# Four staging tiles instead of two for the first eight quarters of V, two of them on the still unused bytes of C

## The chip, the cores and the metric

The kernel runs on one core of one Trainium2 chip. The metric is device time in microseconds (us) of one execution, lower is better. "Faster" or "slower" needs 2%. Where a smaller difference is called one, the 95% interval of its ratio leaves out 1.

The profile names the engines so: PE is TensorE (PEld its weight loads), DVE is VectorE, ACT is ScalarE, POOL is GpSimd, SP is SyncE, which only issues transfers. "ACTq" and "SPq" are transfers being issued by the sequencers of ACT and SP. The "granted clock" is the share of TensorE's full clock that the profile says it was given.

## The reference, cut to what matters

Two independent blocks, each on a sequence of 2048 x 1024, are computed and put side by side: a state-space recurrence (A), and attention over segments with a memory (B). Only one product matters here, V of block B:

```python
def _B_ref(x, mem0, Wq, Wk, Wv, Wo, seg_len):      # x: 1 x 2048 x 1024, 32 heads of 128
    ...
        v = jnp.einsum('btd,dhe->bhte', h, Wv)      # V: 1024 x 4096 weights
    ...
```

and of block A, that its output needs the matrix C, a second 1024 x 1024 complex product, only after the whole recurrence input has been computed:

```python
    Bu = jnp.einsum('bld,pd->blp', x + 0j, B_bar)
    ...                                             # the recurrence over 2048 steps
    y = 2.0 * jnp.einsum('blp,dp->bld', hseq, Cmat).real + x * Dskip[None, None, :]
```

## The kernel before

V is computed first, in 8 blocks of four heads (`hb`), each in four quarters (`q`) of 512 rows. A quarter is four tiles of 128 rows; a tile is eight accumulating matmuls of 128x512 into one PSUM buffer (where TensorE leaves its results). ScalarE copies ("evicts") the four tiles into a staging tile in SBUF (the memory on the core), and one DMA then writes the staging tile to DRAM (`b_vx`), from where attention reads it much later.

```python
    def ps(self, tag, shape=(128, 512), dt=FP32):
        ...  bufs={"P": 3, "S": 2, "R": 1, "O": 2, "U": 2}[tag]     # three PSUM buffers "P"

    def stage_init(self):
        self.vst = []
        for i in range(2):
            self.vst.append(self.wl.tile([128, 4, 4, EW], BF16, name=f"b_vst{i}", bufs=1))
            self.k.G.memset(self.vst[i][:, :, :, E:EW], 1.0)
        self.nst = 0

    def next_st(self):
        self.nst += 1
        return self.vst[self.nst % 2]

    def v_x(self, hb, q, w):
        ...
        st = self.next_st()
        ...
        for i in range(4):
            ...
                p = k.ps("P")[:]
                self.v_mm(p, w, 4 * q + i)                          # 8 matmuls
            k.copy("v" if first and i % 2 else "s", st[:, i, :, 0:E], p.rearrange(...))   # "s": ScalarE
        ...
        Q.dma_start(vx[s0:s0 + n * 128, :].rearrange(...), st[:, 0:n, :, :].rearrange(...))
        ...
```

The order of the first work items is V quarters (0,0), (1,0), (0,1), (1,1), with nothing between them; from then on one step of the state-space block (16 matmuls into a "U" buffer, 3.45 us of TensorE) stands between two quarters in most places. While the first V quarters run, ScalarE also builds sine and cosine tables for the state-space block, and SP loads `x` of both blocks by transposing DMAs.

The staging tile of quarter n is that of quarter n-2. So the first eviction of a quarter has two conditions: TensorE must have finished the tile, and the DMA that wrote quarter n-2 to DRAM must have landed.

The space for C is a tile of its own, `a.CT` (named `t32`, in the profile `t`), 32 KB per partition. It is allocated at the start and written from 208 us on.

## Time and profile before

| | before |
|---|---|
| time, median of 3 | 1247.49 us (1247.30 to 1248.05) |
| span of the profiled execution | 1245.6 us |
| TensorE busy | 1234.4 us, 99% |
| ScalarE busy | 263.5 us, 21% |
| DMA share, 20 to 40 us | 1.17 to 1.24 |
| granted TensorE clock | 1.000 |

The DMA share is the mean busy share of the 16 DMA engines. The times of all packets are added up, so a share above 1, as here, means that packets overlapped on an engine.

From the page of the kernel before: the span, the busy line, and the chain of work that ended last by engine.

```profile
span 1245.6 us, 20120 instructions
...
PE 1234.4 (99%) x8270; PEld 662.3 (53%) x8342; DVE 668.0 (54%) x1250; ACT 263.5 (21%) x631; POOL 275.8 (22%) x407
...
PE 98%; DMA 1%; issue 0%; ACT 0%; POOL 0%; DVE 0%; SPq 0%; ACTq 0%
```

The timeline of TensorE in the stretch of the change (start, length, engine, line, operation, output<-inputs, sizes, number of instructions; idle time before a group would stand at the end in brackets):

```profile
15.20 20.92 PE L64 MATMUL psP<-b_wv,b_xe 128*128 128x512 bf16 x94
35.96 3.62 PE L64 MATMUL psU<-a_xT,a_bt 128*128 128x512 bf16 x16
39.41 7.07 PE L64 MATMUL psP<-b_wv,b_xe 128*128 128x512 bf16 x31
```

Twelve V tiles, 96 matmuls (two records are missing), start at 15.20 us, and the next group starts at 35.96: 20.76 us, 216 ns per matmul, 1.73 us per tile, no bracket anywhere. A group's printed length (20.92) reaches past the start of the next group because matmuls are pipelined and their ends are modelled; the starts are what to subtract.

The timeline of ScalarE around the fourth quarter (L89 is the copy helper, L494 the issue of the write):

```profile
24.96 0.57 ACT L89 ACTIVATE b_vst<-psP 128x512 bf16<-128x512 f32 x1
25.43 0.62 ACT L238 ACTIVATE a_tabh<-a_tabh 128x512 bf16<-128x512 bf16 x1
25.56 0.37 ACTq L494 DMA_DIRECT2D b_vx<-b_vst  x1
...
30.20 0.37 ACTq L494 DMA_DIRECT2D b_vx<-b_vst  x1
32.75 1.08 ACT L89 ACTIVATE b_vst<-psP 128x512 bf16<-128x512 f32 x2 [1.97 <-PE psP L64]
...
39.43 0.37 ACTq L494 DMA_DIRECT2D b_vx<-b_vst  x1
```

At 25.56 us the write of the second quarter is issued. The first eviction of the fourth quarter, which goes into the same staging tile, starts at 32.75 us after 1.97 us of idle ScalarE. The bracket blames TensorE, but TensorE had finished that tile at about 15.20 + 9 x 1.73 = 30.8 us, and an eviction that waits only for TensorE starts within about 0.2 us of the end of its tile. So the other condition, the landing of the write, must have been the late one. That is a reading.

TensorE's own waits up to 200 us (waiter, what it waited for, us in total, times, longest):

```profile
PE psR L64 <- DVE hpb L105: 1.3, 1, 1.3
PE psP L64 <- ACT b_xe L89: 0.2, 1, 0.2
```

Neither is an eviction of V.

### The profile page before, as it was taken

How to read it: one execution, taken by the hardware profiler on the slowest of the kernel's cores; microseconds unless marked ns; L12 is line 12 of the kernel's file. 1: busy time of each engine (PE TensorE's matmuls, PEld its weight loads, DVE VectorE, ACT ScalarE, POOL GpSimd, SP SyncE). 2: the span in 40 equal slices, each digit the busy share in tenths (PEclk: the TensorE clock that was granted, in tenths of full speed). 3: DMA queues.
4: the chain of work that ended last, by engine and by line, in shares of the span. 5: the costliest groups of instructions: out<-in, count | busy, mean ns of one | idle time of the engine just before them, and what ended most of it. 6: DMA issues, size and time to landing. Idle time of an engine off the chain costs nothing.

```text
span 1245.6 us, 20120 instructions
## 1 busy us (share of the span) xinstructions
PE 1234.4 (99%) x8270; PEld 662.3 (53%) x8342; DVE 668.0 (54%) x1250; ACT 263.5 (21%) x631; POOL 275.8 (22%) x407
## 2 busy tenths in 40 slices
PE   9999999999999999999999999999999999999998
PEld 5444444444455555556666656555665554446444
DVE  4688899998711124666666666666666641001000
ACT  5344444443310000211112111111211110000000
POOL 4111331212332321322222222222222220000000
PEclk9999999999999999999999999999999999999999
DMA  9965444554898834664454544545473289407000
GB/s 245 272 192 148 131 132 128 144 156 107 241 323 247 251 116 95 192 167 123 95 144 108 144 108 114 138 92 133 96 155 95 61 223 220 110 18 153 17 17 27
DMA packets 316022, 176.83 MB, mean 142 GB/s; under 512 B 138650, under 2 KB 301326, under 8 KB 315926
## 3 DMA queue, kind: packets, MB, share of 16 engines
q1 hardware_dynamic: 293830, 147.95, 48.1%
q10 hardware_dynamic: 21072, 24.38, 5.9%
q0 software_dynamic: 1024, 3.17, 0.7%
q8 instruction: 66, 1.08, 0.4%
q14 instruction: 30, 0.25, 0.1%
HBM read 89.14 MB, written 53.17 MB: 114 GB/s over the span
## 4 chain that ended last, share of the span: by engine, by line
PE 98%; DMA 1%; issue 0%; ACT 0%; POOL 0%; DVE 0%; SPq 0%; ACTq 0%
PE psP L64 82%; PE psU L64 9%; PE psS L64 3%; PE psO L64 2%; PE psR L64 2%; DMA wo<-in_B_Wo_dram 1%; DMA b_xr<-in_B_x_dram 0%; ACT b_xe L89 0%; POOL b_m L644 0%; DVE b_ost L91 0%; SPq L64 0%; ACT b_e L641 0%; ACTq L89 0%
## 5 line engine op out<-in xcount | busy, mean ns | idle before, releaser
L64 PE MATMUL psP<-b_xe,b_wq 128*128 128x480 bf16 (+1 forms) x1280 | 247.7, 343 | 0.1
L64 PE MATMUL psP<-b_xe,b_wk 128*128 128x480 bf16 (+1 forms) x1280 | 247.7, 343 | 0.0
L64 PE MATMUL psP<-b_wv,b_xe 128*128 128x512 bf16 (+2 forms) x1033 | 223.4, 372 | 1.0 <-ACT b_xe L89 0.2
L644 POOL TENSOR_TENSOR b_m<-b_e,maskB 99x396 bf16<-99x396 bf16 x160 | 139.8, 874 | 334.0 <-ACT b_e L641 334.0
L641 ACT ACTIVATE b_e<-psS 99x396 bf16<-99x396 f32 x176 | 88.2, 501 | 532.2 <-PE psS L64 527.9
L64 PEld LDWEIGHTS <-b_wk 128*128 128x128 bf16 x1280 | 119.4, 98 | 94.2
L64 PEld LDWEIGHTS <-b_wq 128*128 128x128 bf16 x1280 | 118.7, 98 | 87.7
L64 PEld LDWEIGHTS <-b_xe 128*128 128x128 bf16 x1056 | 101.8, 98 | 119.1 <-ACT b_xe L89 0.4
L91 DVE CAST b_k<-psP 128x480 bf16<-128x480 f32 (+1 forms) x192 | 97.5, 529 | 101.1 <-PE psP L64 101.1
L91 DVE CAST b_q<-psP 128x480 bf16<-128x480 f32 (+1 forms) x192 | 97.5, 529 | 93.0 <-PE psP L64 91.4
L64 PEld LDWEIGHTS <-b_ol 128*128 128x128 bf16 x864 | 84.3, 98 | 94.4
L64 PE MATMUL psU<-a_xT,a_bt 128*128 128x512 bf16 x493 | 113.9, 379 | 1.1
L64 PE MATMUL psP<-t,a_hl 128*128 128x512 bf16 x496 | 112.1, 379 | 0.8
L91 DVE CAST b_ost<-psP 128x512 bf16<-128x512 f32 (+1 forms) x17 | 11.5, 676 | 183.4 <-PE psP L64 182.4
L64 PE MATMUL psP<-wo,b_ol 128*128 128x512 bf16 (+1 forms) x440 | 91.9, 364 | 0.4
L64 PE MATMUL psP<-t,b_ol 128*128 128x512 bf16 x408 | 91.7, 379 | 0.4
L280 POOL TENSOR_SCALAR a_tt<-a_pr,a_tabf 128x1 f32<-128x1 f32 x48 | 34.1, 709 | 243.5 <-DVE a_pr L275 243.5
L89 ACT ACTIVATE b_vst<-psP 128x512 bf16<-128x512 f32 x126 | 72.0, 589 | 71.0 <-PE psP L64 65.0
L661 DVE TENSOR_TENSOR b_ob<-psO,b_accR 99x384 bf16<-99x384 f32 x160 | 85.9, 553 | 2.0
L267 DVE TENSOR_TENSOR a_pr<-psU,a_tabf 128x2048 f32<-128x2048 f32 x32 | 73.0, 2282 | 15.7 <-PE psU L64 14.0
L64 PEld LDWEIGHTS <-a_bt 128*128 128x128 bf16 x512 | 49.2, 98 | 57.6
L64 PEld LDWEIGHTS <-a_hl 128*128 128x128 bf16 x512 | 49.1, 98 | 56.7
(200 smaller groups left out, 963.8 us busy)
## 6 DMA issues: line engine op xcount, KB each, us to landing
b_v<-b_vx SPq DMA_DIRECT2D x16, 1122.0 KB
b_wv<-in_B_Wv_dram SPq DMA_DIRECT2D x16, 1024.0 KB
b_on<-b_ob SPq DMA_DIRECT2D x15, 960.0 KB
b_vx<-b_vst ACTq DMA_DIRECT2D x24, 544.0 KB
a_hs<-a_h SPq DMA_DIRECT2D x32, 256.0 KB
b_wog<-in_B_Wo_dram SPq DMA_DIRECT2D x4, 2048.0 KB
b_wq<-in_B_Wq_dram SPq DMA_DIRECT2D x16, 512.0 KB
b_wk<-in_B_Wk_dram SPq DMA_DIRECT2D x16, 512.0 KB
```

The costliest lines, as they stand in the source:

```text
L64: r = f(*a, **kw)
L89: self.S.activation(out, in_, ACT.Copy)
L91: self.V.tensor_copy(out, in_)
L267: V.tensor_tensor(pr[:], u[:].unsqueeze(1).to_broadcast([128, 2, 2, TB]), view(t3, [[TB + 1, 2], [TB + 1, 2], [1, TB]]), ALU.mult)
L280: G.tensor_scalar(tt[:, j:j + 1], w[:, j, TB - 1:TB], t3[:, 1, TB:TB + 1], None, ALU.mult)
L641: k.S.activation(e[:], s[0:GW, :, :, 0:GW], ACT.Exp, scale=float(E) ** -0.5, accum_out=self.accE[0:GW, i:i + 1])
L644: k.G.tensor_tensor(m[0:GW, 0:4 * GP].rearrange("p (a b q) -> p a b q", a=2, b=2)[:, :, :, 0:GW], e[:], mask[0:GW, :, :].unsqueeze(2).to_b ...
L661: V.tensor_tensor(self.ob[:, b0:b0 + n, :], o[0:GW, 0:n, 0:E], r.unsqueeze(2).to_broadcast([GW, n, E]), ALU.mult)
```

## The change

Its intent: the early evictions of V shall not wait for the writes of earlier quarters. Two more staging tiles would not need new space: the bytes of C lie idle until long after the first eight quarters. So the first quarters rotate over four tiles, two of them views of C, and from the eighth on over the old two.

```diff
-    def stage_init(self):
-        self.vst = []
-        for i in range(2):
-            self.vst.append(self.wl.tile([128, 4, 4, EW], BF16, name=f"b_vst{i}", bufs=1))
-            self.k.G.memset(self.vst[i][:, :, :, E:EW], 1.0)
+    def stage_init(self, ct):
+        self.vst = [self.wl.tile([128, 4, 4, EW], BF16, name=f"b_vst{i}", bufs=1)[:] for i in range(2)]
+        spare = [ct[:, 1, 4 * i:4 * i + 3, :].rearrange("p c d -> p (c d)")[:, 0:16 * EW].rearrange("p (i h e) -> p i h e", i=4, h=4)
+                 for i in range(2)]
+        self.sts = self.vst + spare
+        for st in self.sts:
+            self.k.G.memset(st[:, :, :, E:EW], 1.0)
         self.nst = 0
     def next_st(self):
         self.nst += 1
-        return self.vst[self.nst % 2]
+        return self.sts[self.nst % (4 if self.nst < 8 else 2)]
...
-            b.stage_init()
+            b.stage_init(a.CT)
```

(One more line, cut here, drops a `[:]` where the two old tiles are used again later.) The instructions of TensorE, VectorE, ScalarE and SP keep their order, apart from those that only wait; GpSimd gets two more memsets.

More of the change, by code (lines that the diff above doesn't have):

```diff
@@ L728, in load_o_early @@
         elif q == 2:
-            t = [v[:].rearrange("p i h e -> p (i h e)")[:, 0:2048].rearrange("p (h n) -> p h n", h=4) for v in self.vst]
+            t = [v.rearrange("p i h e -> p (i h e)")[:, 0:2048].rearrange("p (h n) -> p h n", h=4) for v in self.vst]
         else:
```

## The prediction

> **What bounds the kernel now.** TensorE. The busy table gives PE 1234.4 us of a 1245.6 us span (99%), granted clock 1.00; the chain that ended last is 98% PE. Where the change acts, the PE timeline is one unbroken stream: from 15.20 to 35.96 us twelve V tiles of eight 128x512 matmuls, 20.76 us for 96 matmuls, 216 ns each, and the same pace on to 100 us. The Trainium skill ("TensorE: Matmul & The Clock Gate", "Back-to-back issue gap") states this pace for back-to-back 128x512 matmuls, so no stall hides inside the modelled "busy". PE's waits up to 200 us are 1.3 us at the warm-up and 0.2 us for ScalarE's copy of x; none names a staging tile.
>
> **What the change removes.** An eviction of V into a staging tile waits until the DMA that last read it has landed: with two tiles that of the quarter before last, with four (first eight quarters) four back. By the instruction orders, PE, DVE, ScalarE and SP keep theirs; only waits differ. ScalarE's timeline shows where the wait bites: the fourth quarter's first eviction starts at 32.75 us after 1.97 us idle. Its PSUM was complete at about 30.8 us, and evictions elsewhere start 0.2 us after the last matmul, so about 1.75 us is the write issued at 25.56 us, which took about 7.1 us to land. The page charges the idle to PE. The third quarter starts right behind its predecessor on ScalarE (26.03), the fifth to eighth 0.2 us after PE. So one wait of 1.75 us goes, off PE.
>
> **Is it on the critical path?** No. There are three "P" PSUM buffers. The late eviction frees its buffer at 33.3 us; PE needs it for that quarter's fourth tile at 29.08 + 3 x 1.73 = 34.3 us. 1 us of slack is left, and PE shows no gap. The gain is 0, or a few tenths in an execution where that write lands over 1 us later.
>
> **What it adds.** Two GpSimd memsets (0.21 us each) before the iota, which then ends near 5.8 instead of 5.43 us; its reader on DVE starts at 6.37 us behind a copy, with 2.5 us idle after it. Cost 0. The transposed load of C into those bytes gets waits on ScalarE and GpSimd work of the first 70 us, but is issued after 200 us. Cost 0. Bytes moved: unchanged.
>
> The Trainium skill ("DMA: Bandwidth & Descriptors", "Anatomy of one DMA") puts most of a DMA's fixed cost of about 2 us into completion. Here a staging write took about 7 us while the DMA share is over 1.0 (20 to 40 us): the reuse wait is real, but not binding.
>
> **Predicted.** 1247.4 us, within 1246.5 to 1248.5; chances: faster by over 2% 0.01, within 2% 0.98, slower 0.01.
>
> **What would show each step.** Right: the fourth quarter's first eviction starts near 31.0 us, ScalarE's idle before it near 0.2 us; the PE timeline from 15 to 100 us is the same to 0.1 us; the span is within 0.5 us of 1245.6. Wrong: a new PE wait on a "psP" buffer, or twelve tiles taking other than 20.76 us.
>
> **What would make it wrong.** The profiled execution hiding a stall that timed ones have (their spread is only 0.75 us), or a shifted DMA colliding with the loads of x at 30 to 50 us.

## The result, and the profile after

| | before | after |
|---|---|---|
| time, median of 4 | 1247.47 us (1247.30 to 1248.05) | 1247.18 us (1246.98 to 1247.52) |
| span of the profiled execution | 1245.6 us | 1245.5 us |
| TensorE busy | 1234.4 us | 1234.3 us |
| ratio after / before | | 0.9997 (95%: 0.9980 to 1.0014) |

A ratio here is the mean time of one kernel's runs over that of the other's runs of the same rounds, so it is not quite the ratio of the medians.

From the page of the kernel after, the lines shown of before:

```profile
span 1245.5 us, 20119 instructions
...
PE 1234.3 (99%) x8270; PEld 662.2 (53%) x8342; DVE 667.7 (54%) x1250; ACT 263.6 (21%) x631; POOL 276.2 (22%) x409
```

TensorE's timeline after:

```profile
14.99 20.92 PE L64 MATMUL psP<-b_wv,b_xe 128*128 128x512 bf16 x94
35.75 3.62 PE L64 MATMUL psU<-a_xT,a_bt 128*128 128x512 bf16 x16
39.20 7.07 PE L64 MATMUL psP<-b_wv,b_xe 128*128 128x512 bf16 x31
```

ScalarE's timeline after (the write's line is L496 now; `t` is a staging tile on the bytes of C):

```profile
24.75 0.58 ACT L89 ACTIVATE t<-psP 128x512 bf16<-128x512 f32 x1
...
25.35 0.37 ACTq L496 DMA_DIRECT2D b_vx<-t  x1
...
29.99 0.37 ACTq L496 DMA_DIRECT2D b_vx<-t  x1
30.77 0.60 ACT L89 ACTIVATE b_vst<-psP 128x512 bf16<-128x512 f32 x1 [0.20 <-PE psP L64]
32.50 0.60 ACT L89 ACTIVATE b_vst<-psP 128x512 bf16<-128x512 f32 x1 [1.13 <-PE psP L64]
...
39.42 0.37 ACTq L496 DMA_DIRECT2D b_vx<-b_vst  x1
```

The change did what it was meant to do. The fourth quarter's first eviction moved from 32.75 to 30.77 us, and the idle time before it from 1.97 to 0.20 us. TensorE's stream is the same, gapless 20.76 us as before (14.99 to 35.75). Even the write of the fourth quarter gained nothing: it is issued at 39.42 us against 39.43, although its last eviction ended at 36.55 instead of 36.76 us; the instruction order shows a wait for an earlier transfer ahead of it in both kernels.

The whole stream starts 0.21 us earlier than before. That needs a control, since nothing in the change should do it. Two more things are to be tested: that the wait was for the write, and that what made it worthless is the spare time of the three PSUM buffers, and not a cost that the change brought with it.

### The profile page after: what moved, and what is told of

Same layout as the page of the kernel before. It is cut to its first block, busy times and chain, and to the rows that moved or that the text cites. A ratio compares the mean times of both kernels' runs of the same rounds, so it can differ in the third digit from the quotient of the medians.

```text
span 1245.5 us, 20119 instructions
## 1 busy us (share of the span) xinstructions
PE 1234.3 (99%) x8270; PEld 662.2 (53%) x8342; DVE 667.7 (54%) x1250; ACT 263.6 (21%) x631; POOL 276.2 (22%) x409
## 3 DMA queue, kind: packets, MB, share of 16 engines
q8 instruction: 66, 1.08, 0.4%
## 4 chain that ended last, share of the span: by engine, by line
PE 98%; DMA 1%; issue 0%; ACT 0%; POOL 0%; DVE 0%; SPq 0%; ACTq 0%
PE psP L64 82%; PE psU L64 9%; PE psS L64 3%; PE psO L64 2%; PE psR L64 2%; DMA wo<-in_B_Wo_dram 1%; DMA b_xr<-in_B_x_dram 0%; ACT b_xe L89 0%; POOL b_m L646 0%; DVE b_ost L91 0%; SPq L64 0%; ACT b_e L643 0%; ACTq L89 0%
## 5 line engine op out<-in xcount | busy, mean ns | idle before, releaser
L89 ACT ACTIVATE b_vst<-psP 128x512 bf16<-128x512 f32 x110 | 62.9, 589 | 57.2 <-PE psP L64 48.8
```

The source lines that it names most:

```text
L89: self.S.activation(out, in_, ACT.Copy)
```

## The experiments

Three theories stood against each other.

- **Mine:** the removed wait was real, and on the second quarter's write alone, but off TensorE's path. The late eviction still frees its PSUM buffer before TensorE wants it again. What is left between the two is the *slack*.
- **Rival 1:** the wait was on the path and its removal gained about 1.75 us, but the added memsets took it back.
- **Rival 2:** the profiled execution isn't typical; in timed ones the wait costs TensorE something.

All twelve runs below gave the reference's result. Times are medians; "unchanged" is the kernel before, run in the same set on the same chip.

### The unchanged kernel once more

No edit.

> Control, the unchanged kernel once more. Every theory: ratio 1.000 within 0.001, medians 1247.0 to 1248.1 us. It shows how far the start of the first dense V tile (15.20 us before, 14.99 us in the changed kernel) moves by itself: my theory says by 0.1 to 0.3 us, with the landing of the first loads of x, so that the 0.2 us by which the changed kernel started earlier is not the change. A rival that gives these 0.2 us to the change expects 15.20 again. ScalarE's first eviction of the fourth quarter again about 1.7 us late, 1.5 to 2.2 us idle before it.

Measured: 1247.30 us (1247.06 to 1248.24, 5 runs) against 1247.17 us (9 runs), ratio 1.0002. The stream of V started at 14.78 us, earlier than in either kernel above, and took 20.77 us. So the 0.21 us by which the changed kernel started earlier lie within what the unchanged kernel does by itself. (It moved by 0.42 us, more than the 0.1 to 0.3 expected; that the first loads of x move it was not tested.) The late eviction was there, and now the profile names the write:

```profile
32.94 1.08 ACT L89 ACTIVATE b_vst<-psP 128x512 bf16<-128x512 f32 x2 [2.58 <-DMA b_vx<-b_vst]
```

The idle time of 2.58 us is longer than the 1.5 to 2.2 us expected. In this execution the write took 7.79 us (issue at 25.15, eviction at 32.94) and left much less slack than the first profile suggested; the table below has it.

### The changed kernel, two more sets

No edit.

> The changed kernel once more, with more rounds. My theory (the removed wait is off TensorE's path): ratio to before 0.9995 to 1.0003, a difference of at most 0.4 us either way. Rival (the wait hits the timed executions but not the profiled one): about 1 to 1.75 us faster, ratio 0.9986 to 0.9992. In the trace the fourth quarter's first eviction has about 0.2 us idle before it and twelve V tiles take 20.76 us.

Measured: 1247.62 us (1247.22 to 1247.64, 5 runs) against 1247.17 us (9 runs), ratio 1.0002 (0.9988 to 1.0016). The medians differ by 0.45 us, the changed kernel being the slower, a little more than the 0.4 expected. The idle time before the fourth quarter's first eviction was again 0.20 us, the twelve tiles took 20.77 us.

> The changed kernel a third time, beside more executions of the unchanged one. My theory: the unchanged kernel now and then (some 1 in 6 so far: 4 of 25 above 1247.7 us) runs 0.5 to 1.5 us longer, when the write lands later than the slack of 0.2 to 1.1 us; the changed kernel never does (9 executions so far at or below 1247.64). So again none above 1247.8 here, and one to three such in the unchanged kernel's runs of this set; the medians within 0.4 us. Rival (those long runs have another cause): as many in the changed kernel.

Measured: 1247.15 us (1246.80 to 1248.16, 5 runs) against 1247.60 us (1246.82 to 1247.82, 9 runs), ratio 0.9999. The medians are as expected, but the guess about the rare long executions failed: one of the five of the changed kernel took 1248.16 us, and of the unchanged kernel's nine only one passed 1247.8, at 1247.82. The rare executions that are about 1 us longer have at least one other cause. What it is stays open. One long execution was profiled, the 1247.85 us of the next section. Its twelve tiles took 20.76 us as always; it lost 0.5 us much later, where attention's first product with V (`b_v`) starts 0.69 us after the start of the group ahead of it, against 0.18 us in the kernel before (492.05 and 492.23 us):

```profile
491.99 0.34 PE L64 MATMUL psS<-b_q,b_k 128*128 128x99 bf16 x4
492.68 0.50 PE L64 MATMUL psO<-b_v,b_m 128*128 128x129 bf16 x6 [0.35 <-issue]
```

So in this one the extra time doesn't lie in the stretch of the change.

How far is Rival 2 excluded? A single interval does not exclude it (that of the first set reaches down to 0.9980, or -2.5 us). But the means of the changed kernel in the three sets lie -0.35, +0.27 and -0.18 us from those of the unchanged one, and over all of them its 14 executions average 0.04 us less than the 22 beside them, with a standard error of 0.1 us (our sums). A gain of 1 us in the usual execution would show. Also, in all runs but the first the profiled execution is itself one of the timed ones, and no profile of an eviction of normal length on two tiles has a stall in these twelve tiles.

### What the change adds, alone

All four tiles are set up, but only the first two are used:

```diff
-        return self.sts[self.nst % (4 if self.nst < 8 else 2)]
+        return self.sts[self.nst % 2]
```

> Only what the change adds: all four tiles are set up (four memsets) but the quarters still alternate over two. My theory: the same time as before within 0.4 us, and the late eviction is back (1.5 to 2.2 us idle on ScalarE before the fourth quarter's first eviction). Rival (a gain of about 1.75 us was given back by the added memsets and the later iota): 1.5 us slower than before.

Measured: 1247.36 us (1247.24 to 1247.85, 4 runs) against 1247.17 us, ratio 1.0001. The late eviction is back:

```profile
32.67 1.09 ACT L89 ACTIVATE b_vst<-psP 128x512 bf16<-128x512 f32 x2 [1.95 <-PE psP L64]
```

None of the four executions is near 1.5 us slower; the longest, by 0.7 us, is the one whose extra time was found above at 492 us. So the additions can't have eaten a gain of 1.75 us: Rival 1 falls.

### Three tiles

```diff
-        return self.sts[self.nst % (4 if self.nst < 8 else 2)]
+        return self.sts[self.nst % (3 if self.nst < 8 else 2)]
```

> One extra staging tile in place of two. My theory: only the write of the second quarter is in the way of the fourth, so three tiles remove the wait as wholly as four: 0.2 us idle before the fourth quarter's first eviction, PE stream unchanged, same time within 0.4 us. Rival (several quarters wait and the fourth tile has a part in it): an idle stretch of over 0.3 us with a landed DMA behind it remains before some first eviction of quarters four to seven.

Measured: 1247.36 us (1247.06 to 1247.62, 4 runs) against 1247.17 us, ratio 1.0000. The fourth quarter's first eviction:

```profile
30.91 0.60 ACT L89 ACTIVATE b_vst<-psP 128x512 bf16<-128x512 f32 x1 [0.20 <-PE psP L64]
```

One extra tile removes the wait as wholly as two.

### One tile

Of the kernel before, the opposite direction:

```diff
-        return self.vst[self.nst % 2]
+        return self.vst[0]
```

> The opposite direction: one staging tile for all quarters, so every quarter's first eviction waits for the write just before it. My theory (the reuse wait is on the write's landing, about 7 us in this stretch, and three PSUM buffers absorb only what stays within a quarter): TensorE stalls by some 3 to 6 us in each of the second to fourth quarters, nothing or little later where a state-space step of 3.45 us lies between quarters; total 1262 us (1255 to 1270). Rival (evictions do not really wait for the landing, the trace only looks so): 1247.5 us. Rival (the reuse wait hurts wherever it is met): over 28 quarters about 3 us each, above 1300 us.

Measured: 1266.24 us (1265.30 to 1270.09, 4 runs) against 1247.29 us (7 runs), ratio 1.0148 (1.0131 to 1.0165). The profiled execution is the longest of the four. TensorE's timeline of the dense quarters, and of the last quarters:

```profile
15.27 5.35 PE L64 MATMUL psP<-b_wv,b_xe 128*128 128x512 bf16 x24
21.03 1.89 PE L64 MATMUL psP<-b_wv,b_xe 128*128 128x512 bf16 x7 [0.40 <-ACT b_vst L89]
25.40 7.03 PE L64 MATMUL psP<-b_wv,b_xe 128*128 128x512 bf16 x24 [2.48 <-ACT b_vst L89]
33.52 7.07 PE L64 MATMUL psP<-b_wv,b_xe 128*128 128x512 bf16 x31 [1.09 <-ACT b_vst L89]
43.82 3.57 PE L64 MATMUL psP<-b_wv,b_xe 128*128 128x512 bf16 x8 [3.24 <-ACT b_vst L89]
47.19 4.87 PE L64 MATMUL psU<-a_xT,a_bt 128*128 128x512 bf16 x16
...
340.29 12.25 PE L64 MATMUL psP<-b_wv,b_xe 128*128 128x512 bf16 x55
357.91 11.66 PE L64 MATMUL psP<-b_wv,b_xe 128*128 128x512 bf16 x39 [5.37 <-ACT b_vst L89]
```

and the second quarter's first two evictions on ScalarE:

```profile
20.38 0.60 ACT L89 ACTIVATE b_vst<-psP 128x512 bf16<-128x512 f32 x1 [3.00 <-DMA b_vx<-b_vst]
21.00 1.28 ACT L187 ACT_TABLE_LOAD   x1
...
24.77 0.57 ACT L89 ACTIVATE b_vst<-psP 128x512 bf16<-128x512 f32 x1
```

Now TensorE waits for evictions, and ScalarE for writes. The total is in the expected range, so evictions do wait for the landing. The distribution was foreseen only in part. The second quarter's fourth tile is held up for only 0.40 us, the third quarter's for 1.09, the fourth quarter's for 3.24. The 2.48 us ahead of the third quarter's first tile have a second cause, which makes this a less clean experiment than the others. That tile takes the buffer of the second quarter's second tile, whose eviction ends at 24.77 + 0.57 = 25.34 us. In the kernel before, this eviction (18.86 us) comes ahead of ScalarE's table work; in the kernel built from this edit it comes behind 3.8 us of it. So the edit also moved instructions of ScalarE, and how much of the 2.48 us the write alone would cost was not separated. A stretch I had overlooked is at the end: the last three quarters stand back to back again, and there a single stall is 5.37 us. Where a state-space step lies between two quarters TensorE loses almost nothing, as expected: between these two stretches the stream has one gap, of 1.36 us at 228 us.

The gaps of this execution add up to only 13.9 us in the wait view, yet its span is 22.7 us longer (1268.3 against 1245.6). Each bracket leaves out about 0.17 us, by which the modelled end of a group reaches past the start that its successor could have had; that makes 1 us for the six. The rest, nearly 8 us, is mostly a lower clock after gaps: the eight matmuls at 43.82 us take 3.37 us to the next group's start where they would take 1.73. The granted clock was 0.50 from 44 to 48 us. The Trainium skill ("TensorE: Matmul & The Clock Gate", "What's actually happening") tells of a gate that halves the clock after an idle window; 0.50 agrees. (On the length of that window see the end.)

### The slack, by making the fourth quarter's first eviction longer

These kernels measure the slack itself. Only the first eviction of the fourth quarter is changed: one instruction writes 4 or 8 copies of the PSUM tile. The first copy goes where it belongs, the next three to places that later evictions of the quarter overwrite, any more to idle bytes of C, so the result is right. Each number of copies is meant for two and for four staging tiles; both lie on the same code, and the tile of this quarter lies on the bytes of C in both.

```diff
+        self.big = ct[:, 0, 0:5, :].rearrange(...)[:, 0:32 * EW].rearrange("p (i h e) -> p i h e", i=8, h=4)
+        self.k.G.memset(self.vst[0][:, :, :, E:EW], 1.0)
-        self.sts = self.vst + spare
+        self.sts = [self.big[:, 0:4], self.vst[1]] + spare
...
-        return self.sts[self.nst % (4 if self.nst < 8 else 2)]
+        return self.sts[self.nst % M] if self.nst < 8 else self.vst[self.nst % 2]      # M = 2 or 4
...
+            if (hb, q, i) == (1, 1, 0):
+                so, si = self.big[:, 0:N, :, 0:E], si.unsqueeze(1).to_broadcast([128, N, 4, E])   # N = 4 or 8
```

> Two tiles, and the fourth quarter's first eviction made longer: one instruction that writes eight copies, 3.6 us in place of 0.6 (estimate from 0.59 us for 512 and 1.02 us for 1024 elements). My theory of the slack: it starts at about 32.7 us, frees its PSUM buffer at 36.3, TensorE wanted it at 34.3: a stall of 2.1 us (1.6 to 2.6) ahead of that quarter's fourth tile and the time up by as much. Rival (stalls are hidden or other slack exists): no gap, or one of 3.0 us.

> The same eight-copy eviction with four tiles. My theory: it starts at about 30.9 us and frees the buffer at 34.5, a stall of 0.3 us (0 to 0.6), so 1.75 us less than with two tiles: the removed wait becomes visible once the slack is used up. Rival (the wait was never one of ScalarE on the write, or the extra tiles do nothing for it): the same stall as with two tiles.

Measured: with two tiles 1249.28 us (1248.69 to 1251.31, 4 runs), ratio 1.0017 (1.0001 to 1.0034); with four 1247.47 us (1247.39 to 1247.58, 4 runs), ratio 1.0000; unchanged 1247.29 us. TensorE and the long eviction with two tiles:

```profile
14.89 19.20 PE L64 MATMUL psP<-b_wv,b_xe 128*128 128x512 bf16 x86
36.49 1.89 PE L64 MATMUL psP<-b_wv,b_xe 128*128 128x512 bf16 x8 [2.40 <-ACT t L89]
38.22 3.62 PE L64 MATMUL psU<-a_xT,a_bt 128*128 128x512 bf16 x16
...
32.86 3.58 ACT L89 ACTIVATE t<-psP 128x4096 bf16<-128x4096 f32 x1 [2.39 <-DMA b_vx<-t]
```

and with four:

```profile
14.79 19.20 PE L64 MATMUL psP<-b_wv,b_xe 128*128 128x512 bf16 x86
34.20 1.89 PE L64 MATMUL psP<-b_wv,b_xe 128*128 128x512 bf16 x8 [0.22 <-ACT t L89]
35.93 3.62 PE L64 MATMUL psU<-a_xT,a_bt 128*128 128x512 bf16 x16
...
30.57 3.58 ACT L89 ACTIVATE t<-psP 128x4096 bf16<-128x4096 f32 x1 [0.20 <-PE psP L64]
```

The same longer eviction costs TensorE a gap of 2.40 us with two tiles and 0.22 us with four (2.57 and 0.38 us from the starts of the groups, as the brackets leave out 0.17 us each). The busy instructions of ScalarE, VectorE and GpSimd have the same order in both kernels. In both, TensorE goes on 0.05 us after the eviction's end (32.86 + 3.58 = 36.44, then 36.49; 34.15, then 34.20). So TensorE's wait is for this PSUM buffer, and the removed wait becomes visible as soon as the slack is used up.

> Two tiles and four copies, about 1.9 us for the eviction. My theory: the buffer comes free at about 34.6 us, a stall of 0.4 us (0.1 to 0.7); with the eight-copy run this gives the slack of the unchanged kernel, 0.8 to 1.1 us, as the sum of the added time less the stall. Rival: a stall of 1.3 us (no slack) or none (more slack than 1.3 us).

Measured in a single look (state unknown): 1247.25 us. The long eviction ran from 32.23 for 1.88 us, the twelve tiles took 20.91 us, a stall of 0.15 us. That is at the low end of the expected range, since the write landed earlier than usual.

Because the first set showed a spread with two tiles, both eight-copy kernels and the four-copy one were run again with more rounds.

> The eight-copy eviction on two tiles again, for its spread. In the first set its four times ran from 1248.69 to 1251.31 us, those with four tiles from 1247.39 to 1247.58. My theory (the landing of the second quarter's write varies by 1 us and more between executions, and with the slack used up all of that reaches TensorE): again a spread of at least 1 us, median 1.5 to 2.5 us above the unchanged kernel. Rival (the 1251.31 was a one-off of the chip): all times within 0.6 us of each other.

> The same with four tiles: no write to wait for, so no spread. My theory: all times within 0.6 us, median 0.1 to 0.4 us above the unchanged kernel. Rival (one-offs of the chip): the same spread as with two tiles.

> The four-copy eviction on two tiles, timed. It adds 1.28 us, so my theory gives a stall of 0.15 us where the write lands as in the first look and of up to 1.5 to 2 us where it lands late: times from 1247.2 to 1249.5 us, a spread of over 0.8 us, median 0.3 to 1.0 us above the unchanged kernel. Rival (constant landing): all within 0.5 us of 1247.3 us.

Measured, against 1247.60 us unchanged: eight copies on two tiles 1251.72 us (1249.72 to 1252.97), ratio 1.0028 (1.0014 to 1.0042); on four tiles 1247.75 us (1247.37 to 1248.18), ratio 1.0003; four copies on two tiles 1248.24 us (1247.46 to 1248.48), ratio 1.0006. Two tiles show a spread of 3.25 us, four tiles of 0.81 us. The median with two tiles is 4.1 us above the unchanged kernel, more than the 1.5 to 2.5 expected; the spread with four tiles is a little over the 0.6 us expected. In the profiled execution with two tiles the write landed latest of all, and the clock fell:

```profile
14.97 19.20 PE L64 MATMUL psP<-b_wv,b_xe 128*128 128x512 bf16 x86
37.59 3.02 PE L64 MATMUL psP<-b_wv,b_xe 128*128 128x512 bf16 x8 [3.42 <-ACT t L89]
40.40 4.21 PE L64 MATMUL psU<-a_xT,a_bt 128*128 128x512 bf16 x16
...
33.95 3.58 ACT L89 ACTIVATE t<-psP 128x4096 bf16<-128x4096 f32 x1 [3.40 <-DMA b_vx<-t]
```

The eight matmuls after the gap took 2.81 us to the next group's start instead of 1.73; the granted clock from 38 to 42 us was 0.57.

So the spread is not the landing's alone. The nine executions with eight copies on two tiles fall in two groups: five lie 1.4 to 2.5 us above the median of the unchanged kernel, at a mean granted clock of 1.000, four lie 4.0 to 5.4 us above it, at 0.998. In the one of the second group that was profiled the stall is 3.59 us, and the matmuls after it lose 1.7 us more (1.08 in these eight, 0.60 in the next sixteen). That, and not the landing alone, put the median beyond what was expected.

### The slack in numbers

The profiled executions with two to four tiles fit one sum. TensorE wants the buffer for the twelfth tile at the start of the stream plus 11 x 1.73 = 19.03 us. It can have it 0.05 us after the end of the eviction. The landing is counted from the issue of the second quarter's write to the start of the eviction that waited for it. A positive last column is slack, a negative one a stall; the stall in brackets is the measured one, from the starts of the groups.

| execution | tiles, copies | landing, us | eviction: start + length | buffer free | wanted | slack |
|---|---|---|---|---|---|---|
| before | 2, 1 | 7.19 | 32.75 + 0.60 | 33.40 | 34.23 | 0.83 |
| before, again | 2, 1 | 7.79 | 32.94 + 0.60 | 33.59 | 33.81 | 0.22 |
| memsets only | 2, 1 | 7.17 | 32.67 + 0.60 | 33.32 | 34.17 | 0.85 |
| four copies | 2, 4 | 6.90 | 32.23 + 1.88 | 34.16 | 34.00 | -0.16 (0.15) |
| four copies, more | 2, 4 | 7.16 | 32.63 + 1.88 | 34.56 | 34.14 | -0.42 (0.41) |
| eight copies | 2, 8 | 7.61 | 32.86 + 3.58 | 36.49 | 33.92 | -2.57 (2.57) |
| eight copies, more | 2, 8 | 8.62 | 33.95 + 3.58 | 37.58 | 34.00 | -3.58 (3.59) |
| after | 4, 1 | none waited for | 30.77 + 0.60 | 31.42 | 34.02 | 2.60 |
| eight copies | 4, 8 | none waited for | 30.57 + 3.58 | 34.20 | 33.82 | -0.38 (0.38) |

Not in the table are three tiles and the changed kernel's two later executions (2.59 to 2.60 us) and the second one of eight copies on four tiles (-0.38, stall 0.38). The kernel with one tile has several stalls in a row and does not fit a single sum.

The packed trace has a direct proof of which wait this is, though no view prints it: the updates of the semaphore that tells of this write's landing. In all seven executions with two tiles the last of them came 0.08 to 0.09 us before the late eviction started (32.67 us in the kernel before), also where the bracket blames TensorE. In the six with three or four tiles the same write landed 6.17 to 7.81 us after its issue, at 31.39 to 33.18 us, and the eviction had started ahead of it, at 30.47 to 30.91 us. So the write did not become faster; the eviction no longer waits for it.

With two tiles and an eviction of normal length the slack was 0.22 to 0.85 us; with three or four it is 2.60. The landing varied from 6.90 to 8.62 us between executions. With the latest of these landings, the unchanged kernel would have freed the buffer at 33.95 + 0.65 = 34.60 us, 0.6 us late (an estimate from that execution). No profiled execution of it shows such a stall. So the change buys a margin of about 2 us against a late write, worth some tenths in an execution with a very late one (0.6 in this estimate), which the timings don't resolve.

No version found here beats both kernels by more than the noise: TensorE has no idle time left in this stretch that staging could fill.

## Why the prediction was right

The time was predicted as 1247.4 us (1246.5 to 1248.5) and measured as 1247.18; the later sets gave 1247.62 and 1247.15. Point by point:

- **"One wait of 1.75 us goes, off PE."** Right. The idle time went from 1.97 to 0.20 us. That it was a wait for the write was an inference against the profile's own label, and is shown by three tiles (wait gone), memsets alone (wait back), the executions in which the profile names the write, and the write's semaphore. The sum that found it, the end of the tile from TensorE's stream and 0.2 us of usual delay, gave 1.75 us; the change removed 1.77.
- **"1 us of slack is left."** Right in kind; the size was read from one execution. By the finer sum it was 0.83 us there and 0.22 us in the repeated one. It depends on a landing that varies by 1.7 us in the table. That the margin was large enough in every profiled execution was in part luck: 0.22 us is little beside such a spread. The prediction named the risk ("that write lands over 1 us later"), and an execution with such a landing did turn up, in one of the lengthened kernels.
- **"What it adds."** Cost 0 is right: 1.0001 with the additions alone. The iota ended at 5.71 us, with its reader starting at 6.18 us. The first load of C into the borrowed bytes is issued at 210.30 us against 211.07 before.
- **"The PE timeline from 15 to 100 us is the same to 0.1 us", and twelve tiles take 20.76 us.** The length is exactly right; the stream as a whole started 0.21 us earlier. The control shows that the start moves by 0.4 us with no change at all (15.20 and 14.78), so the tolerance, not the reasoning, was too narrow.
- **"A staging write took about 7 us ... real, but not binding."** Right. The Trainium skill ("DMA: Bandwidth & Descriptors", "Anatomy of one DMA") puts most of a fixed cost of about 2 us into completion, for transfers issued from GpSimd; this one is issued from ScalarE. The runs show a landing of 6.90 to 8.62 us for a write of 544 KB in a stretch where the DMA share is above 1; how much of it is queueing was not separated.

What was predicted less well were experiments: where the stalls of the one-tile kernel fall, and how much a lower clock adds to a stall.

## What to carry to other kernels

A wait that a change removes is worth only what remains after the next buffer in the chain has absorbed it: subtract when the consumer wants the buffer from when the producer frees it, and do it in more than one execution, since a transfer's landing can move by more than the slack. To learn whether a wait is hidden or absent, lengthen the suspected link on purpose, with and without the change; the stall that appears tells the slack of that execution to a few hundredths of a microsecond where the total time tells nothing. Then check that the build kept the order of the other instructions, which the one-tile kernel did not. Where the bound engine already runs without a gap, look elsewhere for time, even if another engine's timeline shows an idle stretch with a clear cause.

## What the Trainium skill lacked or had wrong

- "TensorE: Matmul & The Clock Gate", "Back-to-back issue gap": it gives 131 ns per matmul as the sustained spacing of load-weights and matmul pairs at 512 columns, and calls about 216 ns the isolated gap that over-counts. Here a stream of exactly such pairs runs at 216 ns per matmul (20.76 us for 96), with nothing waiting. The page is not of one mind: its section "Wait — 56ns, not 53.3ns?" gives 215.7 ns from start to start for back-to-back matmuls at the full clock, which agrees.
- The same page, "What's actually happening": this section lets the clock fall after an idle window of about 3.4 us. In the one-tile kernel a gap of 2.48 us was followed by a granted clock of 0.73 (24 to 28 us), while a gap of 2.40 us in the eight-copy kernel was not (1.00 from 38 to 42 us). A gap of 3.42 us was followed by 0.57. So a gap shorter than the stated window can cost clock, and not every one does; what decides was not tested.
- "DMA: Bandwidth & Descriptors", "Anatomy of one DMA": its fixed cost of 2.0 us plus size over 436 GB/s, stated for transfers issued from GpSimd, would give an estimate of about 3.3 us for a write of 544 KB. The same write, issued from ScalarE, landed after 6.90 to 8.62 us under load, with a spread of 1.7 us between executions. The page has an HBM access latency at high load (2 us, "Latency and other measured facts"), but no number for the landing of a whole transfer while the engines are busy.
- No page read says how to find the slack behind a buffer wait; here the sum of the table above gave stalls to 0.01 us.
